# Converting the last four weight tiles in two halves each, in an attention and feed-forward kernel

## The chip, the cores and the metric

The kernel runs on one core of a Trainium2 chip. The metric is the device time of one execution in microseconds (us); several runs are taken and their median is compared. The core's engines run side by side, each with its own in-order queue: PE (matrix multiply, with its weight loads shown as PEld), DVE (vector engine), ACT (scalar engine), POOL, and SP, which here only issues DMA transfers.

## The reference

```python
def _attn_ref(q, k, v, phi):                 # (8, 8, 576, 64), phi (8, 8, 576, 32)
    a = softmax(phi, axis=2)
    k_m = einsum('bhsm,bhsd->bhmd', a, k)    # 32 memories for each head
    v_m = einsum('bhsm,bhsd->bhmd', a, v)
    attn = softmax(q @ k_m^T / sqrt(64), axis=-1)
    return attn @ v_m

def _moe_ref(x, w1, w2, w3, w_out):          # x (4608, 512), w1, w2 (512, 1024)
    h = ((x @ w1) * (x @ w2)) @ w3           # w3 (1024, 1024), w_out (1024, 512)
    return h @ w_out
```

The four weights reach the kernel as 64-bit floats, the other arrays as 32-bit ones. The attention output, heads side by side, is the x of the feed-forward part.

## The kernel before, in words

**Weights.** w3 and w_out are multiplied with each other once (`product`, line 386, `keep` on line 400 splits the result into a rounded part Wh and a rest Wl). w1 and w2 are folded with each batch's value memories (`memory_weights`, line 288): `step` for a quarter q of their columns multiplies `w12_sb[q]` by `vm` (line 298) and splits the product into mh and ml. All weights arrive as 64-bit floats and are first turned into 32-bit ones.

**The tiles.** The list `tasks` (lines 321 to 325) holds 22 tiles: numbers 0 to 13 are w3 and w_out, 14 and 15 are quarter 0 of w1 and w2, 16 and 17 quarter 1, 18 and 19 quarter 2, 20 and 21 quarter 3. `fetch(i)` starts the 1 MB transfer of a tile into a raw buffer; `convert(i)` turns it into 32-bit words y with five instructions:

- line 377, DVE: the sign bit into the upper halves of a helper tile u
- line 378, ACT: the high words, scaled, into y
- line 379, ACT: the low words, scaled, into the lower halves of u
- line 381, DVE: y shifted left by 3
- line 382, DVE: y and u added (a custom instruction that the trace counts in 16-bit elements, so 2048 for 1024 words)

Tiles from `FIRST_LATE` = 18 on have no raw buffers of their own. They borrow those of the attention: tile 18 the buffer kv0, 19 kv2, 20 q, and 21 kv0 again, which it can have only when tile 18 has been read. Their helper tiles are al (18 and 20, one buffer after the other) and ua (19 and 21).

**The order.** Lists of step names (START, FIRST, SECOND, STEADY, lines 22 to 37) set the program's order; C is `next_tile`, which converts one tile and fetches a later one, A is `ab_unit`, N a quarter of the first batch's memory weights, W a `product`, K a `keep`, O an `out_part`. PE and SP run in exactly that order. DVE and ACT are put in order by a scheduler when the kernel is built, from the order of the lists, the dependencies and its own estimates. The four late tiles belong to FIRST, which is the first batch.

**The unit.** `ab_unit` (line 437) makes two products a and b on PE, six matmuls each, in two PSUM banks for a and two for b, in turn. ACT copies a out (a_sb, line 458), DVE multiplies b by it (gr, line 460), ACT rounds gr to gh, and DVE takes the rest gl (line 116). PE's b of a unit can start when the gr of the unit two before has emptied its bank.

Of the kernel before, what the change touches and what calls it, by code (L numbers as in the profile page):

```python
# [10 lines left out]
I32 = mybir.dt.int32  # L11
# [29 lines left out]
def memory_attention__then__bilinear_ffn_kernel(  # L41
# [282 lines left out]
    tasks += [("w31", k, 2, rows(w3T[:, DF:], k, 2)) for k in range(0, NF, 2)]  # L324
    tasks += [("w12", (q, i), NG, w[:, :, 2 * q * FQ : 2 * (q + 1) * FQ]) for q in range(NQ) for i, w in enumerate((w1, w2))]
    FIRST_LATE = 18
    CW = DF
    BUFS = 5
    raws, w3s = {}, {}
# [4 lines left out]
    def fetch(i):  # L334
        if i >= len(tasks):
            return
        kind, _, n, src = tasks[i]
        if i < FIRST_LATE:
            raw = init.tile([P, CW * 2], I32, name="raw", bufs=BUFS)
        else:  # L340

            name = ("kv0", "kv2", "q")[(i - FIRST_LATE) % 3]
            shape = [P, NG, S] if name == "q" else [P, 2, 8 * 2 * D]
            raw = att.tile(shape, F32, name=name, tag=name).bitcast(I32)
            raw = raw.rearrange("p a b -> p (a b)")
        words = n * src.shape[2] // 2
        raws[i] = raw[:, : 2 * words].rearrange("p (k x) -> p k x", k=n)
        nc.sync.dma_start(out=raws[i], in_=src)

    def convert(i):  # L350

        kind, at, n, _ = tasks[i]
        raw = raws.pop(i)
        if kind == "w12":
            y = w12_sb[at[0]][:, at[1]]
        elif kind == "wo":
            y = wos[at // half][:, at % half : at % half + n]
        else:
            y = const.tile([P, n, CW // 2], F32, name="w3", tag=f"m{free_m.pop(0)}")
            for j in range(n):  # L360
                w3s[int(kind[2]), at + j] = y[:, j]
        if i < FIRST_LATE:
            u = init.tile([P, CW], I32, name="u", bufs=2)
        elif i % 2:
            u = att.tile([P, 5 * NT * P], I32, name="ua", tag="a")
        else:
            u = att.tile([P, 2, S], F32R, name="al", tag="al", bufs=2).rearrange("p t s -> p (t s)").bitcast(I32)
        x = y.shape[-1]
        u = u[:, : n * x].rearrange("p (k x) -> p k x", k=n)
        halves = u.bitcast(U16).rearrange("p k (x c) -> p k x c", c=2)  # L370
        words = raw.rearrange("p k (x c) -> p k x c", c=2)
        low, high = words[:, :, :, 0], words[:, :, :, 1]
        top = raw.bitcast(U16).rearrange("p k (x c) -> p k x c", c=4)[:, :, :, 3]
        y = y.bitcast(I32)


        nc.vector.tensor_scalar(out=halves[:, :, :, 1], in0=top, scalar1=0x8000, scalar2=None, op0=ALU.bitwise_and)
        nc.scalar.activation(out=y.bitcast(F32), in_=high.bitcast(F32), func=AF.Copy, scale=2.0**-112)
        nc.scalar.activation(out=halves[:, :, :, 0], in_=low.bitcast(U32), func=AF.Copy, scale=2.0**-29)

        nc.vector.tensor_scalar(out=y, in0=y, scalar1=3, scalar2=None, op0=ALU.logical_shift_left)  # L381
        nc.vector.tensor_tensor(out=y, in0=y, in1=u, op=ALU.add)  # L382
# [24 lines left out]
    def next_tile():  # L407
        i = next(todo)
        convert(i)
        fetch(i + BUFS if i + BUFS < FIRST_LATE + 3 else i + 3 if i >= FIRST_LATE else len(tasks))  # L410

# [166 lines left out]
```

## Time and profile before

| | us |
|---|---|
| median of 3 runs | 551.29 (550.37 to 552.06) |
| the profiled execution | 550.54 |
| its span in the trace | 548.7 |
| PE busy | 531.0 |
| DVE busy | 313.4 |
| ACT busy | 249.9 |

The span runs from the first to the last recorded instruction; the 1.84 us between it and the time of the execution lie around it. Busy time is a sum over stages with different limits, so a stretch of the span has to be looked at by itself to see which engine holds it up.

### The profile page before, as it was taken

What the parts mean: (1) busy time and instruction counts of PE and PEld (TensorE: products, weight loads), DVE (VectorE), ACT (ScalarE), POOL (GpSimd) and SP (SyncE); (2) the same over time, 40 slices, a digit from 0 to 9 for tenths busy, and PEclk for the clock granted to TensorE, in tenths of its full rate; (3) what the DMA queues carried; (4) which work ended last, traced back from release to release, by engine and by line L of the source; (5) the groups of instructions that cost most, each with busy time, mean ns of one, the idle gap of its engine ahead of it and who ended that gap; (6) DMA issues with size and microseconds to landing.
All of it is one profiled execution on the core that took longest, in us unless ns stands there. A gap on an engine that the chain in (4) does not pass through costs nothing.

```text
span 548.7 us, 9731 instructions
## 1 busy us (share of the span) xinstructions
PE 531.0 (97%) x4024; PEld 427.6 (78%) x4024; DVE 313.4 (57%) x600; ACT 249.9 (46%) x494; POOL 0.7 (0%) x6
## 2 busy tenths in 40 slices
PE   4899999999999999999999999999999999999997
PEld 1344357976998689968996899869986899689985
DVE  4877999557367715593458425673567045915400
ACT  5886966524554325452544335443544044514310
POOL 0000000000000000000000000000000000000000
PEclk9999999999999999999999999999999999999999
DMA  8999828036334510082007210351012100010011
GB/s 295 410 355 391 305 77 270 33 111 231 113 143 168 174 39 21 1 278 82 20 1 280 81 39 1 151 173 56 2 58 69 39 20 2 21 44 14 1 38 57
DMA packets 24987, 64.05 MB, mean 117 GB/s; under 512 B 1776, under 2 KB 2032, under 8 KB 24944
## 3 DMA queue, kind: packets, MB, share of 16 engines
q1 hardware_dynamic: 24944, 63.45, 32.6%
q8 instruction: 31, 0.51, 0.4%
q14 instruction: 12, 0.10, 0.1%
HBM read 54.00 MB, written 9.44 MB: 116 GB/s over the span
## 4 chain that ended last, share of the span: by engine, by line
PE 89%; DVE 7%; DMA 2%; issue 1%; ACT 1%; SPq 0%; DVEq 0%; ACTq 0%
PE o L472 37%; PE b L449 18%; PE a L449 18%; PE a L298 2%; PE a L392 2%; PE b L392 2%; DMA raw<-in_w3T 2%; DVE w L382 2%; PE o L199 2%; PE x L298 2%; PE x L184 1%; PE b L298 1%; PE x L199 1%; PE x L239 1%; DVE w L381 1%
## 5 line engine op out<-in xcount | busy, mean ns | idle before, releaser
L472 PE MATMUL o<-Wh,gh 128*128 128x512 f32 x288 | 115.4, 401 | 0.0
L472 PE MATMUL o<-Wl,gh 128*128 128x512 f32 x288 | 112.8, 391 | 0.0
L472 PE MATMUL o<-Wh,gl 128*128 128x512 f32 x288 | 112.5, 391 | 0.0
L460 DVE TENSOR_TENSOR gr<-b,a_sb 128x288 f32<-128x288 f32 x128 | 58.6, 458 | 85.9 <-PE b L449 82.0
L115 ACT CAST gh<-gr 128x288 fp32r<-128x288 f32 x128 | 55.4, 433 | 100.3 <-DVE gr L460 100.3
L116 DVE TENSOR_TENSOR gl<-gr,gh 128x288 fp32r<-128x288 f32 x128 | 58.6, 458 | 58.9 <-ACT gh L115 58.5
L449 PE MATMUL b<-ah,mh 128*128 128x288 f32 x256 | 76.0, 297 | 1.8 <-DVE gr L460 1.2
L449 PE MATMUL a<-ah,mh 128*128 128x288 f32 x256 | 77.2, 301 | 0.0
L449 PE MATMUL a<-al,mh 128*128 128x288 f32 x256 | 75.6, 295 | 0.1
L449 PE MATMUL b<-al,mh 128*128 128x288 f32 x256 | 75.5, 295 | 0.0
L449 PE MATMUL a<-ah,ml 128*128 128x288 f32 x256 | 75.3, 294 | 0.0
L449 PE MATMUL b<-ah,ml 128*128 128x288 f32 x256 | 75.3, 294 | 0.0
L472 PEld LDWEIGHTS o<-Wh,gh 128*128 128x128 f32 x288 | 54.1, 188 | 22.6 <-issue 11.9
L490 ACT COPY osb<-o 128x512 f32<-128x512 f32 x31 | 18.2, 586 | 100.1 <-PE o L472 87.4
L472 PEld LDWEIGHTS o<-Wl,gh 128*128 128x128 f32 x288 | 54.1, 188 | 12.4
L472 PEld LDWEIGHTS o<-Wh,gl 128*128 128x128 f32 x288 | 54.1, 188 | 10.9
L458 ACT COPY a_sb<-a 128x288 f32<-128x288 f32 x128 | 50.3, 395 | 3.5 <-PE a L449 3.1
L449 PEld LDWEIGHTS a<-ah,mh 128*128 128x128 f32 x256 | 48.0, 187 | 3.0 <-issue 1.0
L449 PEld LDWEIGHTS b<-ah,mh 128*128 128x128 f32 x256 | 48.0, 187 | 2.5 <-DVE gr L460 1.7
L449 PEld LDWEIGHTS a<-al,mh 128*128 128x128 f32 x256 | 48.1, 188 | 0.7 <-DVE al L116 0.3
L449 PEld LDWEIGHTS b<-ah,ml 128*128 128x128 f32 x256 | 48.2, 188 | 0.0
L449 PEld LDWEIGHTS a<-ah,ml 128*128 128x128 f32 x256 | 48.2, 188 | 0.0
(97 smaller groups left out, 650.8 us busy)
## 6 DMA issues: line engine op xcount, KB each, us to landing
kv<-in_kv SPq DMA_DIRECT2D x16, 1024.0 KB, 7.4
q<-in_qT SPq DMA_DIRECT2D x8, 1152.0 KB, 10.5
out<-osb SPq DMA_DIRECT2D x31, 256.0 KB, 2.0
raw<-in_w3T SPq DMA_DIRECT2D x7, 1024.0 KB, 11.8
ph<-in_phiT SPq DMA_DIRECT2D x8, 576.0 KB, 3.9
raw<-in_w SPq DMA_DIRECT2D x4, 1024.0 KB, 17.6
raw<-in_w_out SPq DMA_DIRECT2D x3, 1024.0 KB, 10.4
kv<-in_w SPq DMA_DIRECT2D x3, 1024.0 KB, 14.5
```

Of the source, the lines that this page charges most:

```text
L115: nc.scalar.copy(out=hi, in_=src)
L116: nc.vector.tensor_tensor(out=lo, in0=src, in1=hi.bitcast(F32), op=ALU.subtract)
L184: nc.tensor.transpose(ps[:, c, t], v["ph"][:, t, at : at + P], ident)
L199: nc.tensor.matmul(ps[t][h * M : (h + 1) * M, : 2 * D], lhsT=v["a"][:, i, t, h * M : (h + 1) * M], rhs=kvt[i][:, (4 * t + h) * 2 * D : (4 ...
L298: nc.tensor.matmul(ps[t][g * M : (g + 1) * M], lhsT=vm[b % 2][d, g], rhs=w12_sb[q][d, :, g], start=True, stop=True,)
L382: nc.vector.tensor_tensor(out=y, in0=y, in1=u, op=ALU.add)
L392: nc.tensor.matmul(pw[r][i], lhsT=x[:, i * P : (i + 1) * P], rhs=wos[k // half][:, k % half], start=k == 0, stop=k == NF - 1,)
L449: nc.tensor.matmul(p, lhsT=x[:, t, w, fc : fc + P], rhs=y[:, n, t * HALF : (t + 1) * HALF], start=i == 0, stop=i == len(todo) - 1,)
L458: nc.scalar.copy(out=a_sb, in_=ps[0])
L460: nc.vector.tensor_tensor(out=gr, in0=ps[1], in1=a_sb, op=ALU.mult)
L472: nc.tensor.matmul(v["p"], lhsT=x[f][:, at : at + P], rhs=y[f // half][:, f % half], start=f == 0 and k == 0, stop=f == NF - 1 and k == 2,)
L490: nc.scalar.copy(out=osb, in_=v["p"])
```

## The change

A constant `HALVES_FROM` = 18 is added. From that tile on, `convert` cuts the tile's four row blocks into two pairs and issues the same five instructions for each pair, through a new function `rounded` that holds what was the end of `convert`. For tiles 0 to 17 nothing changes. Transfers, buffers and PE's and SP's order stay as they were.

```diff
     FIRST_LATE = 18
+    HALVES_FROM = 18
@@ convert(i)
         u = u[:, : n * x].rearrange("p (k x) -> p k x", k=n)
+
+        h = n if i < HALVES_FROM else n // 2
+        for j in range(0, n, h):
+            rounded(i, y[:, j : j + h].bitcast(I32), u[:, j : j + h], raw[:, j : j + h])
+
+    def rounded(i, y, u, raw):
         halves = u.bitcast(U16).rearrange("p k (x c) -> p k x c", c=2)
         words = raw.rearrange("p k (x c) -> p k x c", c=2)
         low, high = words[:, :, :, 0], words[:, :, :, 1]
         top = raw.bitcast(U16).rearrange("p k (x c) -> p k x c", c=4)[:, :, :, 3]
-        y = y.bitcast(I32)
```

The five instructions that follow stand as before, six lines further down (377 becomes 383, 382 becomes 388, 460 becomes 466). DVE and ACT come out in a new order at three places. In the rows, w_2 and w_3 are the quarters 2 and 3 of w1 and w2, and a row with x2 is two instructions.

DVE from the middle of the conversions on, before (kv, q: raw buffers; ss, s_sb, at: the second half of the first batch's softmax):

```order
L263 TENSOR_SCALAR ss_469<-ss_469 128x18
L381 TENSOR_SCALAR w_3_84<-w_3_84 128x1024
L377 TENSOR_SCALAR al<-q 128x1024
L264 RECIPROCAL ss_469<-ss_469 128x18
L382 ISA w_3_84<-w_3_84,al 128x2048
L265 TENSOR_TENSOR s_sb<-s_sb,ss_469 128x576
L381 TENSOR_SCALAR w_3_84<-w_3_84 128x1024
L274 STREAM_TRANSPOSE at<-s_sb 128x576
L116 TENSOR_TENSOR Wl_478<-a,Wh_477 128x512
L116 TENSOR_TENSOR Wl_478<-o,Wh_477 128x512 x2
L116 TENSOR_TENSOR Wl_478<-b,Wh_477 128x512
```

The same place on DVE in the changed kernel:

```order
L263 TENSOR_SCALAR ss_469<-ss_469 128x18
L387 TENSOR_SCALAR w_3_84<-w_3_84 128x512
L383 TENSOR_SCALAR al<-q 128x512 x2
L264 RECIPROCAL ss_469<-ss_469 128x18
L387 TENSOR_SCALAR w_3_84<-w_3_84 128x512 x2
L265 TENSOR_TENSOR s_sb<-s_sb,ss_469 128x576
L388 ISA w_3_84<-w_3_84,al 128x1024 x2
L274 STREAM_TRANSPOSE at<-s_sb 128x576
L116 TENSOR_TENSOR Wl_478<-o,Wh_477 128x512 x2
L116 TENSOR_TENSOR Wl_478<-a,Wh_477 128x512
L116 TENSOR_TENSOR Wl_478<-b,Wh_477 128x512
```

The shift of tile 21 and the add of tile 20 have changed places, and the Wl of bank a comes behind those of the two o banks.

DVE at the first three gr, before (ml: the memory weights of quarter 1):

```order
L116 TENSOR_TENSOR ml_493<-x,mh_492 128x1024
L460 TENSOR_TENSOR gr<-b,a_sb 128x288
L382 ISA w_2_83<-w_2_83,ua 128x2048
L460 TENSOR_TENSOR gr<-b,a_sb 128x288
L116 TENSOR_TENSOR gl_508<-gr,gh_500 128x288
L377 TENSOR_SCALAR ua<-kv_542 128x1024
L162 TENSOR_REDUCE mx<-ph 128x2
L460 TENSOR_TENSOR gr<-b,a_sb 128x288
L382 ISA w_3_84<-w_3_84,ua 128x2048
```

The same place on DVE in the changed kernel:

```order
L116 TENSOR_TENSOR ml_493<-x,mh_492 128x1024
L388 ISA w_2_83<-w_2_83,ua 128x1024
L466 TENSOR_TENSOR gr<-b,a_sb 128x288
L388 ISA w_2_83<-w_2_83,ua 128x1024
L466 TENSOR_TENSOR gr<-b,a_sb 128x288
L116 TENSOR_TENSOR gl_508<-gr,gh_500 128x288
L383 TENSOR_SCALAR ua<-kv_547 128x512 x2
L162 TENSOR_REDUCE mx<-ph 128x2
L466 TENSOR_TENSOR gr<-b,a_sb 128x288
L388 ISA w_3_84<-w_3_84,ua 128x1024 x2
```

Half of the add of tile 19 now stands ahead of the first gr; ahead of the third gr the work is the same as before.

ACT in the same stretch, before (w_2 from kv: tile 19; w_3 from q: tile 20; w_3 from kv: tile 21):

```order
L378 ACTIVATE w_2_83<-kv_345 128x1024
L378 ACTIVATE w_3_84<-q 128x1024
L379 ACTIVATE al<-q 128x1024
L378 ACTIVATE w_3_84<-kv_542 128x1024
L115 CAST Wh_477<-o 128x512 x2
```

The same place on ACT in the changed kernel:

```order
L384 ACTIVATE w_2_83<-kv_345 128x512 x2
L384 ACTIVATE w_3_84<-q 128x512 x2
L384 ACTIVATE w_3_84<-kv_547 128x512 x2
L385 ACTIVATE al<-q 128x512 x2
L115 CAST Wh_477<-o 128x512 x2
```

The high words of tile 21 now stand ahead of the low words of tile 20.

## Rows read from the trace of the kernel before

**Rows 1.** The page, part 1: busy time, share of the span, instructions of each engine.

```profile
PE 531.0 (97%) x4024; PEld 427.6 (78%) x4024; DVE 313.4 (57%) x600; ACT 249.9 (46%) x494; POOL 0.7 (0%) x6
```

**Rows 2.** Busy time by stretch: stretch, length, engines busy, granted clock, DMA.

```profile
60.00:87.40 27.40, 24.56 (x120) 13.70 (x119) 27.38 (x41) 20.03 (x27) 0.00 (x0) 1.00 0.41 143
87.40:546.00 458.60, 457.77 (x3687) 392.03 (x3687) 241.27 (x493) 186.16 (x421) 0.00 (x0) 1.00 0.24 83
```

**Rows 3.** Timeline of PE: start, duration, instruction, in brackets the idle time before it.

```profile
80.45 0.40 PE L449 MATMUL b<-ah,mh 128*128 128x288 f32 x1 [0.53 <-DVE Wl L116]
...
83.25 0.40 PE L449 MATMUL b<-ah,mh 128*128 128x288 f32 x1 [0.57 <-DVE gr L460]
...
87.39 0.40 PE L449 MATMUL b<-ah,mh 128*128 128x288 f32 x1 [0.68 <-DVE gr L460]
...
95.99 1.09 PE L298 MATMUL x<-w,vm 64*32 64x512 f32 x16
```

**Rows 4.** Timeline of DVE around the first three gr.

```profile
82.75 0.45 DVE L460 TENSOR_TENSOR gr<-b,a_sb 128x288 f32<-128x288 f32 x1
83.12 1.21 DVE L382 CUSTOM_DVE_ANT_0 w<-w,ua 128x2048 uint16<-128x2048 uint16 x1
84.25 0.46 DVE L460 TENSOR_TENSOR gr<-b,a_sb 128x288 f32<-128x288 f32 x1
...
85.64 1.34 DVE L162 TENSOR_REDUCE mx<-ph 128x2 f32<-128x1152 f32 x1
86.89 0.45 DVE L460 TENSOR_TENSOR gr<-b,a_sb 128x288 f32<-128x288 f32 x1
87.26 1.22 DVE L382 CUSTOM_DVE_ANT_0 w<-w,ua 128x2048 uint16<-128x2048 uint16 x1
```

**Rows 5.** Lines 377, 381 and 382: count, shortest, median and longest duration in ns.

```profile
L377 DVE TENSOR_SCALAR u<-raw x18: 458/749/767, 4.0 to 63.7; 128x1024 uint16<-128x1024 uint16 x14, 128x512 uint16<-128x512 uint16 x4
L381 DVE TENSOR_SCALAR w<-w x17: 427/689/715, 4.7 to 76.7; 128x1024 int32<-128x1024 int32 x15, 128x512 int32<-128x512 int32 x2
L382 DVE CUSTOM_DVE_ANT_0 w<-w,u x13: 692/1225/1235, 5.4 to 69.1; 128x2048 uint16<-128x2048 uint16 x11, 128x1024 uint16<-128x1024 uint16 x2
```

**Rows 6.** Timeline of DVE while the late tiles are converted.

```profile
68.45 0.78 DVE L377 TENSOR_SCALAR al<-kv 128x1024 uint16<-128x1024 uint16 x1
69.09 1.24 DVE L382 CUSTOM_DVE_ANT_0 w<-w,u 128x2048 uint16<-128x2048 uint16 x1
...
74.55 0.28 DVE L264 RECIPROCAL ss<-ss 128x18 f32<-128x18 f32 x1
74.84 1.23 DVE L382 CUSTOM_DVE_ANT_0 w<-w,al 128x2048 uint16<-128x2048 uint16 x1
...
77.26 0.77 DVE L274 STREAM_TRANSPOSE at<-s_sb 128x576 f32<-128x576 f32 x1
```

**Rows 7.** Timeline of ACT at tiles 20 and 21.

```profile
73.42 1.39 ACT L379 ACTIVATE al<-q 128x1024 uint16<-128x1024 uint32 x1 [3.73 <-DVE ss L263]
74.66 1.15 ACT L378 ACTIVATE w<-kv 128x1024 f32<-128x1024 f32 x1
```

**Rows 8.** Timeline of SP: the issues of tile 21 and of the next phi.

```profile
69.30 0.54 SPq L348 DMA_DIRECT2D kv<-in_w  x1
81.73 0.37 SPq L123 DMA_DIRECT2D ph<-in_phiT  x1
```

**Rows 9.** Transfers issued from 55 to 90 us: count, size, median us to landing.

```profile
kv<-in_kv SPq DMA_DIRECT2D x2, 1024.0 KB, 7.0
...
kv<-in_w SPq DMA_DIRECT2D x1, 1024.0 KB, 5.0
ph<-in_phiT SPq DMA_DIRECT2D x1, 576.0 KB, 3.7
```

**Rows 10.** Line 378 on ACT in sum: count, shortest, median and longest duration in ns.

```profile
L378 ACT ACTIVATE w<-raw x13: 672/1150/1176, 4.0 to 60.5; 128x1024 f32<-128x1024 f32 x11, 128x512 f32<-128x512 f32 x2
```

## The prediction, made before the changed kernel ran

> **What bounds the kernel now.** I read the page first: PE is busy for 531.0 of the span's 548.7 us [rows 1], so anything that doesn't make PE wait is hidden, and anything that does is paid in full. Then the stretches: from 87.40 us to the last matmuls PE is busy for 457.77 of 458.60 us, so no slack is left there to swallow a delay that exists at 87.40, and none to win. In the stretch before it, 60.00 to 87.40, PE is busy for 24.56 of 27.40 us and idle for 2.84, while DVE is busy for 27.38 of 27.40 [rows 2]. This is where the four tiles are converted, and here DVE sets the pace. Third, the timeline of PE, for what it waits on there: a b product waits 0.53 us for a Wl (80.45), 0.57 for the first gr (83.25) and 0.68 for the third gr (87.39), all DVE instructions [rows 3]. The wait that ends last decides: b of the fifth unit at 87.39, released by the gr that DVE starts at 86.89 [rows 4]. From there on PE runs without a gap. So the question is one number: when does DVE reach its third gr in the changed kernel?
>
> **The change part by part.**
>
> *What DVE does ahead of the third gr.* The two orders in the section on the change show that it is the same work: both upper-half writes and shifts of all late tiles, the adds of tiles 18, 19 and 20, the four Wl, al, ml, two gr, one gl and the reduce of phi. Only the add of tile 21 (1.22 us at 87.26 [rows 4]) comes behind it, before and after. No work leaves the stretch. What is new there is that 4 line-377, 4 line-381 and 3 line-382 instructions are cut in two: 11 more starts.
>
> *The price of a start.* From the durations of whole and halved forms [rows 5]: two halves of line 377 last 2 x 458 - 749 = 167 ns longer than the whole, of line 381 2 x 427 - 689 = 165, of line 382 2 x 692 - 1225 = 159. The shown durations overlap, though: the whole line 377 at 68.45 lasts 0.78 us and its successor starts 0.64 later, an overlap of 0.14 [rows 6]; line 382 at 83.12 lasts 1.21 and its successor starts after 1.13, an overlap of 0.08 [rows 4]. I take 0.10, between the two. That leaves about 0.065 us a start, and 11 x 0.065 = 0.7 us. Bounds: with no overlap 11 x 0.163 = 1.8 us; with 0.14 everywhere 11 x 0.024 = 0.26.
>
> The Trainium skill (VectorE: DVE Perf Modes, The DRAIN you can't avoid) says that after each DVE instruction the next does not start until the pipe is empty, and concludes that the number of instructions should be kept small. By that rule the shown durations add up without overlap, and the sum would be the 1.8 us of the upper end. The starts at 68.45 and 69.09 speak against it here, since the second lies 0.14 us ahead of the end of the first [rows 6]; I keep it as a rival below.
>
> *Waits of DVE for ACT.* Two edits of the order touch these. Before, the add of tile 20 starts at 74.84, 0.29 us after a reciprocal of 18 elements at 74.55 [rows 6], just when ACT's low words of that tile end (73.42 + 1.39 = 74.81 [rows 7]): up to 0.15 us of that is a wait, and it goes. In its place ACT now does the high words of tile 21 ahead of the low words of tile 20. Tile 21 sits in kv0, is issued at 69.30, after DVE has read tile 18 there [rows 8], and lands 5.0 us later [rows 9], at 74.3. The halved line 378 lasts 0.67 us [rows 10], so the first half is ready at about 75.0 and the second at about 75.6. DVE, carrying the first five or six starts, wants them at about 75.1 and 75.4: a wait of about 0.2 us on the second half. The low words of tile 20 then run from about 75.5, an estimate of 0.65 us to each half, and are ready at 76.3 and 76.9; DVE comes to that add at 76.6 and 77.2, so it does not wait. New wait and lost wait cancel within 0.1 us: I book zero, with -0.15 to +0.2 as ends.
>
> *Behind it.* ACT's Wh copies queue behind these and end about 1 us later than before. DVE's Wl wants them from about 78.5 on (77.26 + 0.57 for the transpose, plus its 0.7), when the o copies are done, and the a copy about 0.7 us before its turn. So that edit costs nothing while the transfer is on time. Moving the Wl of bank a behind the two of o delays the second unit's a product, and half an add ahead of the first gr delays the third unit's b by some 1.2 us (0.6 for the half add, 0.6 for the starts so far). I cost both at nothing at the end: behind the first gr PE has b, a, b, a of 0.8 us each to do, then stands again before the third gr, and by the sum it reaches that at about 87.65, with the gr ending at 86.89 + 0.7 + 0.45 = 88.04. The cover is 0.4 us; beyond it these edits would be paid too.
>
> *The reduce of phi*, directly ahead of the third gr, starts at 85.64 before [rows 4]; its transfer is issued at 81.73 and lands 3.7 us later, at 85.4 [rows 8, 9]. The issue waits for DVE's al, which moves by 0.6 us, and the reduce moves by 0.7, so the transfer stays just ahead. *Later consumers*: the fourth quarter's weights matmul starts at 95.99 [rows 3], and tile 21's add ends at about 88.5 before; one or two us of delay there are covered by 7. ACT's 8 extra instructions lie in its idle time, which had 3.73 us in one piece ahead of 73.42 [rows 7].
>
> *Sum.* The third gr 0.7 us later, PE 0.7 us later at 87.4, nothing given back in 458 us of full PE: the profiled execution goes from 550.54 to about 551.24, and the median of 551.29, which is 0.75 above that execution, to about 552.0. With the ends of both terms the addition lies between +0.1 and +2.0.
>
> **The rivals.**
>
> *No visible cost.* The overlap of short instructions is the 0.14 us of line 377, the lost wait of 0.15 counts and the new one doesn't: 0.26 - 0.15 = +0.1, so 551.4. For it: nothing but the size of the terms; the same verdict as the forecast.
>
> *No overlap (slower).* Halves of one tile follow each other so closely that their full durations add: 11 x 0.163 = +1.8 us, 553.1. It decides at 1.65 us, that is from 0.15 us a start on. Against it: all neighbours in the rows overlap.
>
> *The transfer of tile 21 (slower).* The new ACT order puts everything on ACT, the low words of tile 20, the Wh, the first a copies, behind one landing at 74.3, where before ACT came to it at 74.66 with 0.3 us in hand [rows 7]. DVE needs the first half by about 75.1, so any delay of the landing beyond 0.1 us is passed on. The neighbouring 1 MB transfers took 7.0 us [rows 9]; with that, 2.0 us more, and the total would be +2.7, or 554.0. It decides against the kernel from a landing 0.95 us later than now. Against it: tile 21 is still issued at 69.3, behind the same DVE read, and the queue is no fuller.
>
> *Earlier release (faster).* Smaller pieces let an urgent gr get in between. The most it could give is the three waits of PE, 0.53 + 0.57 + 0.68 = 1.78 us [rows 3], so 549.5. For it: the second gr now has half an add ahead of it and not a whole one. Against it: the third gr, which ends the stretch, has all the same work ahead, and DVE had 0.02 us of idle time to lose [rows 2]. The Trainium skill (Perfetto Trace Analysis, Optimizing Scalar/DVE Operations) recommends breaking instructions up where Scalar or Vector causes bubbles on other engines without being saturated, and grouping them where it is saturated; by that, this stretch is one for grouping.
>
> **How the numbers follow.** 0.3% of 551.29 is 1.65 us, about what a measurement of this kernel can tell from no change. Forecast (+0.7): 0.63. No visible cost: 0.17. No overlap: 0.08. Late transfer: 0.07. Earlier release: 0.05. Within 0.3% are the first two, 0.80; slower the next two, 0.15; faster the last, 0.05. The three runs before spread by -0.9 and +0.8 around their median, so the range begins at 551.4 - 0.8 = 550.6; at the top it takes in the no-overlap case and half of that spread, 553.1 + 0.5 = 553.6. Left out are the late transfer and the earlier release.
>
> **What would show it.** In the changed profile the halves of lines 377, 381 and 382 should start 0.33 to 0.35, 0.33 and 0.6 us apart; the transpose now at 77.26 should start near 77.8, the third gr near 87.6, and PE's last wait should end near 88.1, with no gap behind it. PE's wait before the third unit's b should grow to about 1.7 us and the one before the fifth unit's b should shrink to about 0.4. The prediction is wrong if the third gr starts earlier than 86.8 (something else held DVE), if a DVE shift of tile 21 waits more than half a microsecond for ACT, or if the third gr is no longer the last thing that PE waits for.

## The result, and the profile after

The changed kernel took 552.40 us (median of 20 runs, 550.49 to 555.12), the kernel before 550.67 (20 runs beside it, 549.67 to 552.28). The ratio is 1.0024 with a 95% interval of 1.0013 to 1.0034, so it is slower by about 1.3 us, between 0.7 and 1.9; the medians alone lie 1.73 us apart. That is inside the 0.3% named as no change. The lowest runs of the two lie 0.82 us apart.

The profiled execution of the changed kernel took 553.15 us, 2.6 more than that of the kernel before (550.54). These 2.6 us have three parts: the first is not due to the change, the second is, and for the third that stays open.

The first part lies ahead of any changed code. The windows of the changed kernel (stretch, length, busy time of PE, PEld, DVE, ACT, POOL, granted clock, DMA share, GB/s), and below them the first window in the kernel before:

```profile
20.00:25.00 5.00, 5.00 (x9) 1.96 (x8) 4.73 (x7) 4.67 (x5) 0.00 (x0) 0.71 1.04 406
...
89.81:546.00 456.19, 456.19 (x3680) 390.92 (x3681) 241.05 (x493) 185.54 (x420) 0.00 (x0) 1.00 0.24 83
```

```profile
20.00:25.00 5.00, 5.00 (x13) 2.25 (x12) 4.73 (x7) 4.73 (x5) 0.00 (x0) 1.00 1.03 403
```

From 20 to 25 us PE was granted 0.71 of its clock; in the kernel before the same stretch has 1.00 and 13 instructions where this one has 9. The timeline of PE there, changed kernel:

```profile
19.50 2.08 PE L398 MATMUL a<-wo,w 128*128 128x512 f32 x2 [2.22 <-DVE wo L388]
21.36 1.81 PE L398 MATMUL b<-wo,w 128*128 128x512 f32 x2
```

and in the kernel before:

```profile
19.58 1.12 PE L392 MATMUL a<-wo,w 128*128 128x512 f32 x2 [2.44 <-DVE wo L382]
20.54 1.02 PE L392 MATMUL b<-wo,w 128*128 128x512 f32 x2
```

The same pair of matmuls starts at about the same time behind about the same idle time, and lasts 2.08 and 1.81 us instead of 1.12 and 1.02. Tiles up to number 17 are converted as before, so no instruction that was changed has run by then; a second profile of the kernel before (below) shows the same loss. DVE comes to tile 18 at 70.08 instead of 68.45 [rows 6], 1.63 us late.

The second part is the change. It is read as a length, which the early lateness doesn't touch: from the upper-half write of tile 18 to the third gr. The timeline of DVE, changed kernel:

```profile
70.08 0.81 DVE L383 TENSOR_SCALAR al<-kv 128x512 uint16<-128x512 uint16 x2
70.76 1.23 DVE L388 CUSTOM_DVE_ANT_0 w<-w,u 128x2048 uint16<-128x2048 uint16 x1
71.89 0.77 DVE L387 TENSOR_SCALAR w<-w 128x512 int32<-128x512 int32 x2
72.56 0.76 DVE L262 TENSOR_REDUCE ss<-s_sb 128x18 f32<-128x576 f32 x1
...
73.89 1.30 DVE L388 CUSTOM_DVE_ANT_0 w<-w,al 128x1024 uint16<-128x1024 uint16 x2
75.09 0.43 DVE L387 TENSOR_SCALAR w<-w 128x512 int32<-128x512 int32 x1
...
76.52 0.27 DVE L264 RECIPROCAL ss<-ss 128x18 f32<-128x18 f32 x1
76.73 1.00 DVE L387 TENSOR_SCALAR w<-w 128x512 int32<-128x512 int32 x2
77.65 0.75 DVE L265 TENSOR_TENSOR s_sb<-s_sb,ss 128x576 f32<-128x576 f32 x1
...
79.52 0.78 DVE L274 STREAM_TRANSPOSE at<-s_sb 128x576 f32<-128x576 f32 x1
...
89.29 0.47 DVE L466 TENSOR_TENSOR gr<-b,a_sb 128x288 f32<-128x288 f32 x1
```

89.29 - 70.08 = 19.21 us, against 86.89 - 68.45 = 18.44 before [rows 4, 6]: 0.77 us more, with 0.7 forecast. With the early 1.63 us taken off, the transpose (79.52) stands at 77.89 where 77.8 was forecast. PE pays the 0.77 us and no more. Its waits in the same stretch:

```profile
82.12 0.40 PE L455 MATMUL a<-ah,mh 128*128 128x288 f32 x1 [1.37 <-DVE Wl L116]
...
86.16 0.40 PE L455 MATMUL b<-ah,mh 128*128 128x288 f32 x1 [1.17 <-DVE gr L466]
...
89.81 0.40 PE L455 MATMUL b<-ah,mh 128*128 128x288 f32 x1 [0.19 <-DVE gr L466]
...
90.81 1.09 PE L298 MATMUL x<-w,vm 64*32 64x512 f32 x16
```

The last wait ends at 89.81, that is 88.18 without the 1.63 of the early lateness, 0.79 behind the 87.39 of [rows 3]. From there to 546.00 PE is busy for all of 456.19 us (the window above), so nothing is given back. The third part is some 0.2 us between 150 and 168 us, where the third batch's phi landed 4.0 us after its issue instead of 3.7. It is taken up again under what is left over.

### The profile page after: what moved, and what is told of

It reads as the page before. It is cut to its first block, busy times and chain, and to the rows that moved or that the text cites. A ratio compares the mean times of both kernels' runs of the same rounds, so it can differ in the third digit from the quotient of the medians.

```text
span 551.4 us, 9751 instructions
## 1 busy us (share of the span) xinstructions
PE 533.4 (97%) x4024; PEld 428.4 (78%) x4024; DVE 314.0 (57%) x612; ACT 249.6 (45%) x502; POOL 0.7 (0%) x6
## 4 chain that ended last, share of the span: by engine, by line
PE 89%; DVE 5%; DMA 3%; ACT 2%; issue 1%; SPq 0%; DVEq 0%; ACTq 0%
PE o L478 36%; PE a L455 18%; PE b L455 18%; PE a L398 2%; PE b L398 2%; PE a L298 2%; DMA raw<-in_w3T 2%; PE o L199 2%; PE x L298 2%; PE x L184 1%; PE b L298 1%; DVE w L388 1%; PE x L199 1%; DMA kv<-in_w 1%; ACT w L384 1%
```

## Experiments

*The stretch* is always the time from the start of tile 18's upper-half write to the start of the third gr: 18.44 us before, 19.21 after. My theory was that extra DVE starts and one new wait for ACT make up its growth; the rivals were full durations without overlap, ACT, the order of the Wl, and, for the 1.6 us at the front, that the change was behind it after all.

### ACT's half of the change alone

In outline:

```diff
+        for j in act:                      # two slices from tile 18 on, one below
+            nc.scalar.activation(out=yi[:, j].bitcast(F32), in_=high[:, j].bitcast(F32), ...)
+        for j in act:
+            nc.scalar.activation(out=halves[:, j, :, 0], in_=low[:, j].bitcast(U32), ...)
```

> Only ACT's two instructions of the late tiles are cut in halves (lines 378 and 379 of before); DVE's three stay whole, and both engines keep the order of the kernel before. Measured from the start of DVE's upper-half write of tile 18 to the start of its third gr (18.44 us before, 19.21 changed). Theory (the cost is DVE's extra starts, 0.065 us each): no extra start on DVE, so 18.4 to 18.6. Rival (halved ACT instructions arrive later and DVE waits for them): 18.8 or more. Rival (the changed kernel's later end comes from the early stage only): 18.4 as well, and the same for every kernel here.

> The kernel with ACT's halves alone again, timed: 8 instructions more than before, all on ACT, the same order and no extra start on DVE. Theory (of the changed kernel's 1.3 us, 0.8 come from DVE's extra starts and the rest from chance events that every kernel has): ratio to before 1.000, within 0.001. Rival (more instructions in the program by themselves make the chance events likelier, a clock loss near 20 us or a late landing of phi near 150 us): ratio 1.001 or more. In the profile: stretch from tile 18's upper-half write to the third gr 18.4 us again.

The stretch was 18.42 us in one execution and 18.44 in the other. DVE's third gr and PE's waits of the first:

```profile
86.82 0.46 DVE L468 TENSOR_TENSOR gr<-b,a_sb 128x288 f32<-128x288 f32 x1
```

```profile
80.40 0.40 PE L457 MATMUL b<-ah,mh 128*128 128x288 f32 x1 [0.54 <-DVE Wl L116]
83.20 0.40 PE L457 MATMUL b<-ah,mh 128*128 128x288 f32 x1 [0.57 <-DVE gr L468]
87.34 0.40 PE L457 MATMUL b<-ah,mh 128*128 128x288 f32 x1 [0.68 <-DVE gr L468]
```

These are the waits of [rows 3], to 0.01 us. Timed, the ratio was 0.9998 (0.9979 to 1.0017, 12 runs at 551.73 us against 20 at 552.03, one of which, of 1839.71 us, the ratio leaves out). ACT's eight extra instructions cost nothing in the stretch, as the step on its idle time had it. The interval is too wide to rule out the rival's 1.001 for the whole execution.

### DVE's half of the change alone

In outline:

```diff
+        for j in dve:                      # two slices from tile 18 on; ACT whole
+            nc.vector.tensor_scalar(out=halves[:, j, :, 1], in0=top[:, j], ...)
+        ...
+        for j in dve:
+            nc.vector.tensor_scalar(out=yi[:, j], in0=yi[:, j], scalar1=3, ...)
+        for j in dve:
+            nc.vector.tensor_tensor(out=yi[:, j], in0=yi[:, j], in1=u[:, j], op=ALU.add)
```

> Only DVE's three instructions are cut in halves, ACT's two stay whole. Same stretch, tile 18's upper-half write to the third gr. Theory: 11 extra starts of 0.065 us, 0.7 us, plus the wait of tile 21's shift for a whole high-words instruction on ACT (which stands ahead of tile 20's low words here too), about 0.4 us: 19.4 to 19.6. Rival (ACT's halves cost it): 18.5. Rival (no overlap between halves, 0.163 us a start): 20.3.

The stretch was 87.89 - 68.61 = 19.28 us, so DVE's half is all of it. That is 0.1 us below the 19.4 to 19.6 expected, since the wait for ACT was shorter than the 0.4 us put down for it. It is one of the rows:

```profile
75.57 0.76 DVE L388 TENSOR_SCALAR w<-w 128x512 int32<-128x512 int32 x2 [0.26 <-ACT w L384]
...
87.89 0.46 DVE L468 TENSOR_TENSOR gr<-b,a_sb 128x288 f32<-128x288 f32 x1
```

ACT does tile 21's high words in one piece here, ahead of tile 20's low words, and DVE waits 0.26 us for them. The whole execution took 553.15 us; what it lost beyond the stretch came later, from a late phi (below).

### Two tiles of the four

```diff
-    HALVES_FROM = 18
+    HALVES_FROM = 20
```

> Tiles 20 and 21 alone by halves, 18 and 19 whole; the order of DVE and ACT is the one of before, so no edit of the order is in it. Ahead of the third gr there are 5 extra starts. Theory: 18.44 + 0.3 = 18.75 us for the stretch, PE's wait ahead of the fifth unit's b about 1.0 us instead of 0.68, and ahead of the third unit's b about 0.7 instead of 0.57. Rival (the edits of the order carry the cost, not the starts): 18.45. Rival (no overlap): 19.25.

```diff
-        h = n if i < HALVES_FROM else n // 2
+        h = n // 2 if i in (18, 19) else n
```

> Halves for tiles 18 and 19 alone; tiles 20 and 21 whole. VectorE has 6 more starts in the stretch, and ScalarE comes to the low words of tile 20 behind the whole high words of tile 21. Theory (starts of 0.06 each, and a wait of VectorE for tile 21's whole high words of 0.3 to 0.45): stretch 18.44 + 0.35 + 0.3 to 0.45 = 19.1 to 19.25. Rival (starts alone decide): 18.8.

Tiles 20 and 21 alone gave 86.86 - 68.33 = 18.53 us, 0.1 more than before where I had expected 0.3: five starts of 0 to 0.07, less the wait for ACT that goes. PE's waits before the third and the fifth unit's b, expected at 0.7 and 1.0, were 0.56 and 0.73; the execution took 552.18 us, with a late phi (below). Tiles 18 and 19 alone gave 87.53 - 68.37 = 19.16. The timeline of DVE shows the wait that belongs to it:

```profile
75.39 0.69 DVE L387 TENSOR_SCALAR w<-w 128x1024 int32<-128x1024 int32 x1 [0.41 <-ACT w L384]
...
87.53 0.46 DVE L466 TENSOR_TENSOR gr<-b,a_sb 128x288 f32<-128x288 f32 x1
```

Six starts at about 0.05 and a wait of 0.41 make the 0.72: it is not starts alone (18.8). The Wl of bank a stands ahead of those of the o banks here, as before, so their order isn't what lengthens the stretch. This is also the cleanest price at the end. The execution had a clock of 1.00 from 20 to 25 us and no late phi, and took 551.25 us against 550.54, 0.71 more. The third gr is 0.64 us later (87.53 against 86.89: the 0.72 of the stretch, less 0.08 by which tile 18 came earlier), and the third quarter's weights matmul 0.65 (89.04 against 88.39). Some 0.1 us was added between 151 and 163 us, where the third batch's phi took 3.9 us instead of 3.7. So, to within 0.1 us, what is lost in this stretch is lost at the end.

### Four pieces instead of two

```diff
-        h = n if i < HALVES_FROM else n // 2
+        h = n if i < HALVES_FROM else n // 4
```

> Late tiles in four pieces each. 33 extra starts ahead of the third gr, and by its order two quarter adds of tile 21 and one more gl stand there too (about 0.7 and 0.4 us). Theory: 33 x 0.065 + 1.1 = 3.2 us more, a stretch of 21.7 us, and since the third gr still decides, a time 3 us over the kernel before (ratio 1.0055). Rival (no overlap): 33 x 0.163 + 1.1 = 6.5 us, stretch 24.9, ratio 1.012. Rival (smaller pieces let an urgent gr in between, since the first two gr come ahead of tile 19's add here): PE's waits shrink, ratio 1.000 or below.

The timeline of DVE:

```profile
67.85 0.72 DVE L383 TENSOR_SCALAR al<-kv 128x256 uint16<-128x256 uint16 x3
...
87.97 1.35 DVE L162 TENSOR_REDUCE mx<-ph 128x2 f32<-128x1152 f32 x1 [0.23 <-DMA ph<-in_phiT]
89.24 0.42 DVE L388 CUSTOM_DVE_ANT_0 w<-w,ua 128x512 uint16<-128x512 uint16 x1
89.57 0.45 DVE L466 TENSOR_TENSOR gr<-b,a_sb 128x288 f32<-128x288 f32 x1
```

The stretch was 89.57 - 67.85 = 21.72 us, 3.28 more. Of that, 0.23 is a wait for phi and about 1.0 is work that now stands ahead of the third gr (two quarters of tile 21's add at 0.33 and one gl at 0.37). The other 2.0 us are 33 starts, 0.06 each. Without overlap 33 starts at the 0.163 of the prediction would have been 5.4 us. The timed ratio, 1.0093 (1.0066 to 1.0120; 555.80 us, 4 runs), is larger than the stretch alone makes it. In the profiled execution PE was granted 0.89 of its clock from 60 to 92 us, after three idle pieces of 1.27, 0.39 and 0.93 us, which I had not foreseen. But that doesn't explain the ratio: the weights matmul started at 91.06, 2.67 us later than before, which is the 3.28 of the stretch less 0.60 by which tile 18 came earlier, and the execution took 553.29 us, 2.75 more than before. The other three took 555.58 to 557.11; where they lost the rest is open.

### Another 1.25 us off DVE

If DVE's work ahead of the third gr sets the end, taking the reduce of phi (1.35 us) out of there must help, and nothing of the change is needed for it.

```diff
-A C C phi1 A A A A C K10 N C kv1 q1 A A ...
+A C C A A A A C K10 N C kv1 phi1 q1 A A ...
```

> The kernel before with the load of the second batch's phi issued behind that of its k and v. The reduce of phi (1.25 us of DVE) then comes behind the third gr, and nothing else ahead of it changes. Theory (the third gr is the wait that ends last, and DVE sets it): the third gr 1.25 us earlier, 17.2 us after tile 18's upper-half write; PE's wait ahead of the fifth unit's b, 0.68 us, disappears and PE is 0.68 us earlier from there on: ratio 0.9988. Rival (another wait takes its place, as the later softmax of phi or the fourth gr): PE is at most 0.2 us earlier, ratio 0.9997 or above.

The same edit on the changed kernel:

> The changed kernel with the same later load of phi. Theory: the third gr no longer decides; PE's last wait is then the one for the first gr (86.16 in the changed kernel, 83.25 before), which half an add of tile 19 and the extra starts delay. PE loses its wait of 0.19 us and no more; beside the kernel before with the later load it stays 1.2 to 1.4 us behind, measured from tile 18's upper-half write to the matmul of the third quarter's weights (line 298). Rival (the extra starts ahead of the third gr are all that counts): it stays 0.8 us behind.

And in place of it, phi between the first and the second of the k and v loads (phi1 leaves its place in the list, and):

```diff
+            if b == 1 and i == 0:
+                load_phi(b)
```

> The kernel before, with the load of the second batch's phi (576 KB) issued between the first and the second load of k and v instead of ahead of both, so that tile 18's and later weights and phi share the queue otherwise; the reduce of phi then stands behind several gr in VectorE's order. My theory (VectorE sets TensorE's last wait of this stage, one reduce of 1.35 us less ahead of the third gr is 1.25 us of its row): third gr about 1.25 us earlier, L298 0.7 to 0.96 us earlier (at 87.4 to 87.7), phi landed by about 92 so that VectorE does not stand still for it as it did with phi behind both loads, ratio 0.998 to 0.9985. Rival: a new wait for phi or a lower clock after new gaps of TensorE takes the gain back, ratio 1.000 or above.

DVE with phi behind both loads, and then between the loads:

```profile
68.47 0.76 DVE L377 TENSOR_SCALAR al<-kv 128x1024 uint16<-128x1024 uint16 x1
...
85.61 0.45 DVE L460 TENSOR_TENSOR gr<-b,a_sb 128x288 f32<-128x288 f32 x1
...
97.84 1.35 DVE L162 TENSOR_REDUCE mx<-ph 128x2 f32<-128x1152 f32 x1 [2.82 <-DMA ph<-in_phiT]
```

```profile
68.27 0.74 DVE L379 TENSOR_SCALAR al<-kv 128x1024 uint16<-128x1024 uint16 x1
...
85.39 0.45 DVE L462 TENSOR_TENSOR gr<-b,a_sb 128x288 f32<-128x288 f32 x1
...
93.42 1.35 DVE L164 TENSOR_REDUCE mx<-ph 128x2 f32<-128x1152 f32 x1 [1.97 <-DMA ph<-in_phiT]
```

At the place the theory held: stretches of 17.14 and 17.12 us, PE's wait before the fifth unit's b gone, the next weights matmul at 87.43 and 87.21 instead of 88.39:

```profile
88.39 1.09 PE L298 MATMUL x<-w,vm 64*32 64x512 f32 x16
```

In total it failed. DVE takes its instructions in order, and now stands 2.82 and 1.97 us at a phi that has not landed; the gr behind it come late, and PE waits for them. With phi behind both loads PE waits 0.90 us for a gr (at 99.61) and then 1.76 for a_sb, and has 0.83 of its clock from 100 to 110 us. With phi between the loads there is one such wait:

```profile
95.19 0.40 PE L451 MATMUL b<-ah,mh 128*128 128x288 f32 x1 [1.11 <-DVE gr L462]
96.18 1.09 PE L300 MATMUL x<-w,vm 64*32 64x512 f32 x16
```

The weights matmul at 96.18 is 0.19 behind that of [rows 3]: 1.18 us of gain at 87.21 (0.18 of it from an earlier tile 18), gone 9 us later. The timed ratios were 1.0058 (1.0036 to 1.0081, 8 runs) and 1.0034 (1.0016 to 1.0053, 12 runs). Neither beats the kernel before. On the changed kernel the edit moved the third gr out of the way too, and PE's weights matmul still stood 88.09 - 67.96 = 20.13 us after tile 18's start, 1.17 behind the same edit on the kernel before (87.43 - 68.47 = 18.96). That is the delay at the earlier waits, half an add and the starts ahead of the first gr, which the changed kernel hides behind its third gr; without that cover it is paid.

### Early tiles halved

```diff
-        h = n if i < HALVES_FROM else n // 2
+        h = n // 2 if i in (4, 5) else n
```

> The late tiles whole as before, and tiles 4 and 5 in two halves: the conversion ahead of PE's longest early wait (2.44 us before the matmuls at 19.58 us). PE can start on the first halves about 1.5 us earlier. Theory (from 45 to 60 us the transfers and DVE set the pace, so the early gain is lost again; what remains is a shorter idle time, after which the clock is less often at its lower level): the third quarter's weights matmul starts within 0.3 us of before (88.4) in an undisturbed run, ratio 0.998 to 1.000. Rival (PE's early wait is on the path): that matmul 1.0 to 1.5 us earlier and ratio 0.9975. Rival (the extra starts on DVE cost more than that): ratio above 1.0005.

```profile
18.16 1.12 PE L398 MATMUL a<-wo,w 128*128 128x512 f32 x2 [0.73 <-DVE wo L388]
...
61.83 1.09 PE L298 MATMUL x<-w,vm 64*32 64x512 f32 x16 [2.91 <-DVE w L388]
...
84.71 0.61 PE L455 MATMUL b<-ah,mh 128*128 128x288 f32 x1 [3.12 <-DVE Wl L116]
```

PE starts 1.42 us earlier at 18.16 and then waits 2.91 us for the first weights (0.95 before), so that gain is gone at 61.83. The third quarter's weights matmul, expected within 0.3 us of 88.4, came at 91.98. So the loss behind the ratio of 1.0056 (1.0021 to 1.0092, 5 runs) has another source in the profiled execution: DVE's instructions came out in an order with the reduce of phi ahead of the Wl of bank b, PE waited 3.12 us for it, and worked at 0.58 of its clock from 84 to 88. A run with a new order elsewhere doesn't price halves.

### Both kernels once more

> The kernel before once more, as a second profile beside the changed one. Theory: stretch from tile 18's upper-half write to the third gr 18.4 us; granted clock in 20 to 25 us either 1.00 (L298 near 88.4, time near 550.5) or 0.7 (L298 near 90, time near 552.3), since the early loss is not the change's. Rival: the stretch itself scatters by several tenths, and then 0.8 us of the changed kernel is not told from it.

> The changed kernel once more. Theory (the change costs about 0.8 us between tile 18's upper-half write and the third gr, and the 1.6 us that the first profile was late before it was by chance, from the clock between 20 and 25 us): the stretch is 19.1 to 19.3 us again whatever the clock does early; where the granted clock in 20 to 25 us is 1.00, L298 is at about 89.2 and the time near 551.2; where it is 0.7, L298 is near 90.8 and the time near 553. Rival (the early loss belongs to the change): granted clock 0.7 again, time near 553.

The kernel before, unchanged: one window, DVE's stretch and third-batch phi, and PE's wait for the latter.

```profile
20.00:25.00 5.00, 5.00 (x9) 2.03 (x8) 4.73 (x7) 4.68 (x5) 0.00 (x0) 0.66 1.03 405
```

```profile
69.98 0.74 DVE L377 TENSOR_SCALAR al<-kv 128x1024 uint16<-128x1024 uint16 x1
...
88.36 0.45 DVE L460 TENSOR_TENSOR gr<-b,a_sb 128x288 f32<-128x288 f32 x1
...
151.80 1.35 DVE L162 TENSOR_REDUCE mx<-ph 128x2 f32<-128x1152 f32 x1 [2.17 <-DMA ph<-in_phiT]
```

```profile
155.20 0.40 PE L449 MATMUL a<-ah,mh 128*128 128x288 f32 x1 [1.22 <-ACT a_sb L458]
```

The changed kernel:

```profile
20.00:25.00 5.00, 5.00 (x9) 2.09 (x8) 4.73 (x7) 4.70 (x5) 0.00 (x0) 0.66 1.03 404
```

```profile
70.15 0.81 DVE L383 TENSOR_SCALAR al<-kv 128x512 uint16<-128x512 uint16 x2
...
89.30 0.45 DVE L466 TENSOR_TENSOR gr<-b,a_sb 128x288 f32<-128x288 f32 x1
```

The stretch repeats: 88.36 - 69.98 = 18.38 us before, 89.30 - 70.15 = 19.15 after, again 0.77 apart. And the kernel before lost its early clock here too (0.66), so the first of the three parts of the 2.6 us isn't the change's. It also had the late phi, and took 553.44 us, more than either profile of the changed kernel (553.15 and 553.12). This pair alone, 553.44 before and 553.12 after, without its traces, would have told the wrong sign.

## Why the prediction was right

**The place.** The forecast took DVE's third gr as the one event that matters. It held in all ten profiles in which the load of phi and the early tiles were left alone: the third quarter's weights matmul starts 1.48 to 1.52 us after the third gr in each of them, and the end follows (0.64 us at the third gr, 0.71 at the end with tiles 18 and 19). None of the three signs of being wrong showed.

**The number.** That the forecast median of about 552.0 lies only 0.4 us from the 552.40 measured is in part luck. It stood on a median of 551.29 from three runs, 0.62 above the 550.67 of the 20 runs. What was forecast is the addition, 0.7 us: the stretch bears it out with 0.77, and the timed runs give 1.3 (0.7 to 1.9).

**The starts.** The forecast was 11 starts at 0.065 us, 0.7 us. The rows after give 0.68 us for a pair of line 383 where the whole took 0.64, 0.67 for a pair of line 387 where it took 0.60, and 1.20 for a pair of line 388 where it took 1.13: 0.04, 0.07 and 0.07 a start, with 4, 4 and 3 of them 0.65 us. The 0.60 is read from the kernel before:

```profile
70.22 0.71 DVE L381 TENSOR_SCALAR w<-w 128x1024 int32<-128x1024 int32 x1
70.82 0.77 DVE L262 TENSOR_REDUCE ss<-s_sb 128x18 f32<-128x576 f32 x1
```

Quarters give 0.06 again. The bound without overlap fell with them. The Trainium skill (VectorE: DVE Perf Modes, The DRAIN you can't avoid) has the next instruction wait until the pipe is empty, and, in a last clause that the prediction left out, start earlier where it isn't held. As the prediction read the first half, the shown durations would have added up to the 1.8 us, and the trace disagrees (0.77). The advice to keep the number of operations small, which the Trainium skill gives on the same page (VectorE: DVE Perf Modes, Rules for kernel authors), agrees with the trace: each start did cost 0.04 to 0.07 us.

**The waits for ACT.** Booked at zero from a new wait of 0.2 and a lost one of up to 0.15. Measured: DVE's pair of shifts at 76.73 takes 0.92 us to the next start instead of 0.67, a wait of 0.25; the add that stood 0.29 us after the reciprocal [rows 6] is replaced by a shift 0.21 after it, 0.08 gained. The sum is +0.17, inside the ends that were given, not zero. 0.65 + 0.17 is 0.82, against 0.77 measured; the 0.05 between them is the size of the rounding in the rows.

**The cover.** The edits of the order were costed at nothing at the end, with 0.4 us in hand before the fifth unit's b. The end was right, but the way was not: I had not priced the Wl of bank a as a wait of its own. It was the longest of the stretch (1.37 us at 82.12), the third unit's b then waited 1.17 instead of the 1.7 named, and only 0.19 us of cover was left. With the cover taken away the delays ahead of the third gr are paid, as the two kernels with phi later show (1.17 us). A smaller slip: the transpose at 77.26 was given 0.57 us, and its successor starts 0.69 later (77.95); nothing else in the sum hung on it.

**The transfers.** Tile 21 and the second batch's phi stayed on time: no DVE row of the stretch waits for a DMA in the changed kernel. Tile 21 landed 5.0 us after its issue as before, and ACT took it up at once:

```profile
76.01 1.26 ACT L384 ACTIVATE w<-kv 128x512 f32<-128x512 f32 x2 [4.67 <-DMA kv<-in_w]
```

DVE's wait of 0.25 us for ACT stands behind this landing, as the prediction's step on it has it; that step foresaw 0.2. So the rival of the late transfer fell. The rival of the earlier release fell with PE's three waits, 1.78 us together before [rows 3] and 2.73 after. The Trainium skill (Perfetto Trace Analysis, Optimizing Scalar/DVE Operations) would group instructions on a saturated engine, and names about 60 ns of access overhead for each DVE instruction on SBUF; DVE had 0.02 us to lose here, and the runs agree with both (0.04 to 0.07 us a start).

**What is left over.** The ratio makes the difference 1.3 us (0.7 to 1.9), the stretch explains 0.8. The other 0.5 may be no more than scatter: 0.8 is within the interval. If it is real, the runs speak against the lost clock as its source. The mean granted clock of whole executions was 0.997 or less in 5 of the changed kernel's 20 runs and in 14 of the 43 of the kernel before for which it is recorded in the later comparisons, so a lost clock was not commoner after the change. And the runs of 0.999 or more lie 1.3 us apart by themselves: 15 of the changed kernel have a median of 551.96, and 29 of the kernel before, not run beside them, 550.64.

The third batch's phi may account for some of it. It landed 5.2 to 5.5 us after its issue in 5 of the 14 traces, of kernels with hardly any delay (18.53 and 18.38 us) as well as with one (19.28). In the other nine it took 3.7 or 3.8 us where the stretch was 18.44 or less (four traces) and 3.9 or 4.0 where it was longer (five, both of the changed kernel among them). So some 0.2 us more may follow from the change; by what way isn't shown. Whether the change also makes the late landing likelier was not settled, since it can't be told without a trace of each run.

## What to carry to other kernels

Cutting an instruction in two on an engine with no idle time costs one start for each cut (here 0.04 to 0.07 us), and a cut can bring a new order and a new wait with it (here 0.25 us). The start is read from the distance between two starts, not from the durations. A wait that is hidden because another comes later is still there: look for what would be paid if the later one went. Measure an effect of 0.1% as the length of its own stretch between two events of the trace, since events elsewhere in an execution set two profiles of the same kernel 2.9 us apart (550.54 and 553.44).

## What the runs showed of the hardware

**The clock after idle time.** Between 18 and 20 us PE starts again, in ten of the 14 profiled executions after 2.2 to 3.0 us of idle, in the other four after 0.7 to 1.9. In four of the ten the matmuls behind it then took up to 1.9 to 2.1 us a pair instead of 1.02, with a granted clock of 0.66 to 0.71 from 20 to 25 us, part of that time at 1.2 GHz and the rest at 2.4; in the others it was 1.00, 2.4 GHz throughout. Among the ten the length of the idle time doesn't tell them apart: 2.22, 2.37, 2.85 and 2.98 us went before a loss, 2.44, 2.57, 2.73, 2.82, 2.86 and 3.01 before none. The loss cost 1.5 to 1.9 us, read at the first weights matmul (62.79 to 63.20 us instead of 61.30). Over the 43 later executions of the kernel before, 29 with a mean of 0.999 or more have a median of 550.64 us, and 14 at 0.997 or less one of 552.83 (one run of 1839.71 us is left out).

**One transfer, two times.** The third batch's phi, 576 KB, landed 3.7 us after its issue in the profile of the kernel before, and in its second profile 5.2 after. The DMA issues from 140 to 156 us, first and second profile:

```profile
ph<-in_phiT SPq DMA_DIRECT2D x1, 576.0 KB, 3.7
```

```profile
ph<-in_phiT SPq DMA_DIRECT2D x1, 576.0 KB, 5.2
```

Same kernel, same bytes, and 1.4 us at the end, since DVE stands in front of it (2.17 us at 151.80 above). What delays it is open.
